# Splitting the level update of the first two tiles between VectorE and GpSimd in a linear-attention and GELU kernel

## The chip, the cores and the metric

The kernel runs on one core of one Trainium2 chip. The time is device microseconds of one execution. Five engines work side by side, each on its own queue of instructions in program order: TensorE (PE, whose weight loads are listed apart as PEld), VectorE (DVE), ScalarE (ACT), GpSimd (POOL) and SyncE (SP, which here only issues DMAs). They wait for each other through semaphores.

## The reference

Linear attention with decay per channel (4 batches, 8 heads, 768 positions, 48 channels), whose output feeds two matrix products with an exact GELU between them (3072 tokens, 384 to 2048 to 384):

```python
for t in range(S):
    kt, vt, rt, wt = (k[:, :, t], v[:, :, t], r[:, :, t], w[:, :, t])
    cur = np.einsum('bhd,bhe->bhde', u[None] * kt, vt)
    y[:, :, t] = np.einsum('bhd,bhde->bhe', rt, state + cur)
    state = wt[:, :, :, None] * state + np.einsum('bhd,bhe->bhde', kt, vt)
...
h = x @ w_in
g = 0.5 * h * (1.0 + erf(h * inv_sqrt2))
return (g @ w_out).astype(np.float32)
```

All inputs are float32, `w` lies between 0.8 and 0.95.

## The kernel before, in words

**Tiles.** The work is cut into 8 tiles `x` of 384 positions (a batch has two of them). `attention(x, unit)` makes the attention of a tile, `mlp(x)` its two products. While `mlp(x - 1)` runs, the attention of tile `x` is woven into it; the strings in `PLAN` say, letter by letter, which stream makes its next step, so the order of every engine's queue is written out by hand. In `PLAN[0]` there is no product to weave into: tile 0 runs as two units of half its heads each (streams `.` and `s`), beside the conversion of the weights (`c`) and the loads (`l`).

**Levels.** Inside a chunk of 64 positions the attention matrix is built in levels h = 1, 2, 4, 8, 16, 32 (`halves`, used for tiles 0 and 1 alone; the others use `quarters`). At each level

1. PE makes products `d` of `k` and `r` (L472) into PSUM,
2. `r` and `k` are multiplied in place by products of the decay `w` (`tot[h]`): of each stretch of 2h positions the later half of `r`, the earlier half of `k` (the update, L514 and L525),
3. the part of `d` that belongs to the level is copied into `a_sb`, under a mask by VectorE (L536) or, from h = 16, by ScalarE (L533).

The products of the next level wait for both halves of the update. After each product of tile 0 two matmuls over zeros (`keep_warm`, L242) follow on PE. Past the last level PE transposes `k` (L705), ScalarE copies that out (L707), PE makes `kv` (L731), VectorE chains the states (L746), and PE adds both parts of `y` (L772, L817); that last one reads the updated `r`.

**The update before.** Most updates are one VectorE product over both tensors (L525): the access patterns `rk` and `tt` step over `r` and `k` as an outer dimension of two, since both lie in one buffer (`bufs[0]` for tile 0, `bufs[1]` for tile 1). It takes 128 x 768 elements for a unit of tile 0 and 128 x 1536 for tile 1. In tile 0 at h = 1 and h = 32, `r` and `k` are already two products (L514, 128 x 384 each); that of `r` at h = 32 is put off until after the `kv` matmuls (`last_r`).

**What else is on VectorE there.** The weights arrive as 16 pieces of 64-bit floats. ScalarE makes three passes over each (L350, L351, L352), VectorE three more (L363, L365, L369). All the pieces are converted while tiles 0 and 1 run, and the products of `mlp(0)` (L1079, L1173) use them as they come. ScalarE takes its next piece only when VectorE has given a buffer back, and it also makes the GELU (L1082, L1084) that empties PE's PSUM banks.

**GpSimd** fills buffers and index patterns at the start, then fills `places` (L301, L306: a memset and four copies, into the end of the `w` of tile 0, so they wait for the level h = 1), and from tile 2 on issues DMAs that add (L990).

Of the kernel before, what the change touches and what calls it, by code (L numbers as in the profile page):

```python
# [72 lines left out]
def kernel(  # L73
# [25 lines left out]
    nc = tc.nc  # L99
# [185 lines left out]
    for i, h in enumerate(QUARTERS[:1]):  # L285
        for a in range(3):
            w_q = (3 - a) * C // 4
            z = q_ints[1 if a == 0 else 2]
# [84 lines left out]
    def attention(x, unit):  # L373
# [6 lines left out]
        n_u = qs * T  # L380
        base = unit * 3 * n_u
        r, k, w = (bufs[0 if x == 0 or i == 0 and x % 2 == 0 else 1][:, base + i * n_u:base + (i + 1) * n_u]
                   for i in range(3))
# [43 lines left out]
        for h in LEVELS:  # L427
            nb = n_u // (2 * h)
            t2 = tot[h].rearrange("p (n two) -> p n two", two=2)
# [35 lines left out]
        def products(bs, right, width, rest=False):  # L465
            d = pair("d")
            n = 0
            for b in bs:
                for i in range(NI):
                    for g in range(2):  # L470
                        for p in range(2):
                            nc.tensor.matmul(d[half[p], g, n * width:(n + 1) * width],  # L472
                                             lhsT=kc[half[g], b, i, p], rhs=right(half[g], b, i, p),
                                             start=True, stop=True)
                    n += 1
            if x == 0 and not rest:
                keep_warm(2)
            return d[:, :, 0:n * width]

        def diagonal():  # L480
            return [products([b], lambda z, b, i, p: rucs[b][z, i, p], C) for b in range(np_)]

        def copy_diagonal(diag):
            for b in range(np_):
                nc.vector.copy_predicated(out=at[:, :, b * NI:(b + 1) * NI],
                                          mask=masks[0].unsqueeze(1).unsqueeze(1).to_broadcast([128, 2, NI, C]),
                                          data=diag[b].rearrange("p g (i t) -> p g i t", t=C))

        def halves():

            for h in LEVELS:
                m = C // 2 // h
                if np_ < NPART:

                    d = products(range(np_), lambda z, b, i, p: rc[z, b, i, p], C, h == 1)
                    d = d.rearrange("p g (n m two j) -> p g n m two j", two=2, j=h, m=m)[:, :, :, :, 1, :]
                else:
                    right = rc.rearrange("p b i c (m two j) -> p b i c m two j", two=2, j=h)[:, :, :, :, :, 1, :]
                    d = products(range(np_), lambda z, b, i, p: right[z, b, i, p], C // 2)
                    d = d.rearrange("p g (n m j) -> p g n m j", j=h, m=m)  # L500
                if h == 1:
                    yield
                    diag = diagonal()
                yield

                r2 = r.rearrange("p (n two j) -> p n two j", two=2, j=h)[:, :, 1, :]
                t2 = tot[h].rearrange("p (n two) -> p n two", two=2)[:, :, 0:1].to_broadcast(r2.shape)
                k2 = k.rearrange("p (n two j) -> p n two j", two=2, j=h)[:, :, 0, :]
                tk = tot[h].rearrange("p (n two) -> p n two", two=2)[:, :, 1:2].to_broadcast(k2.shape)
                rk = bass.AP(tensor=r2.tensor, offset=r2.offset, ap=[r2.ap[0], [n_u - h, 2]] + list(r2.ap[1:]))  # L510
                tt = bass.AP(tensor=t2.tensor, offset=t2.offset, ap=[t2.ap[0], [1, 2]] + list(t2.ap[1:]))

                def update(z, r2=r2, t2=t2, k2=k2, tk=tk):
                    nc.vector.tensor_mul(*((k2, k2, tk) if z is k else (r2, r2, t2)))  # L514

                if x == 0 and m == 1:

                    update(k)
                    last_r.append(lambda: update(r))
                elif x == 0 and h == 1:  # L520
                    update(r)
                    yield
                    update(k)
                else:
                    nc.vector.tensor_mul(rk, rk, tt)  # L525
                yield
                ah = at.rearrange("p g n (m two j) -> p g n m two j", two=2, j=h)[:, :, :, :, 1, :]
                if h >= 16:

                    for p in range(2):  # L530
                        for i in range(m):
                            s = slice(p * 64 + i * 2 * h, p * 64 + i * 2 * h + h)
                            nc.scalar.copy(out=ah[s, :, :, i], in_=d[s, :, :, i])  # L533
                else:
                    mask = masks[h].rearrange("p (m j) -> p m j", j=h).unsqueeze(1).unsqueeze(1)
                    nc.vector.copy_predicated(out=ah, mask=mask.to_broadcast(ah.shape), data=d)  # L536
                if h == 1:
                    copy_diagonal(diag)
                yield
# [154 lines left out]

        last_r = []
        yield from halves() if x < 2 else quarters()


# [634 lines left out]
```

## Time and profile before

Three executions took 591.37, 592.99 and 596.03 us, median 592.99. The profiled execution's span is 591.7 us, with a mean granted PE clock of 0.997.

| engine | busy us | share of the span | instructions |
|---|---|---|---|
| PE | 575.3 | 97% | 7536 |
| PEld | 511.1 | 86% | 7536 |
| DVE | 436.3 | 74% | 835 |
| ACT | 281.4 | 48% | 648 |
| POOL | 51.5 | 9% | 57 |

The stages that hold the change, in us from the start of the span: tile 0 from the first product at 9.2 to its last `y` at 43.5, tile 1 from there to about 115. PE is busy for 31.3 of the first 43.5 us and, by the profile, for all of the time from 43.5 to 136.7; a busy PE is not PE at its peak, since matmuls are pipelined. GpSimd is busy for 8.0 us before 19 and for nothing from there to the first adding DMA.

Busy time of a group is listed with its mean for one instruction in ns. "Idle before" is the time that the engine stood still just ahead of these instructions, with what ended it. A wait put down to "issue" is one for which the profile shows no releaser.

### The profile page before, as it was taken

What the parts mean: (1) busy time and instruction counts of PE and PEld (TensorE: products, weight loads), DVE (VectorE), ACT (ScalarE), POOL (GpSimd) and SP (SyncE); (2) the same over time, 40 slices, a digit from 0 to 9 for tenths busy, and PEclk for the clock granted to TensorE, in tenths of its full rate; (3) what the DMA queues carried; (4) which work ended last, traced back from release to release, by engine and by line L of the source; (5) the groups of instructions that cost most, each with busy time, mean ns of one, the idle gap of its engine ahead of it and who ended that gap; (6) DMA issues with size and microseconds to landing.
All of it is one profiled execution on the core that took longest, in us unless ns stands there. A gap on an engine that the chain in (4) does not pass through costs nothing. (4 is left out here: it accounts for less than half of the span.)

```text
span 591.7 us, 17485 instructions
## 1 busy us (share of the span) xinstructions
PE 575.3 (97%) x7536; PEld 511.1 (86%) x7536; DVE 436.3 (74%) x835; ACT 281.4 (48%) x648; POOL 51.5 (9%) x57
## 2 busy tenths in 40 slices
PE   5879999999999999999999999999999999999997
PEld 3566666766799999999999999999999999999997
DVE  6979989998969886786859977686759977420332
ACT  2367889223612458046462368145560466435400
POOL 3100000000000130012100120003100111003100
PEclk8999999999999999999999999999999999999999
DMA  6758581020152532245232533334225232214200
GB/s 237 206 181 309 164 280 62 30 91 1 27 143 78 139 59 43 79 126 89 28 59 86 148 64 50 91 121 55 29 36 160 75 52 35 34 47 53 28 15 33
DMA packets 60797, 53.89 MB, mean 91 GB/s; under 512 B 32304, under 2 KB 45872, under 8 KB 60720
## 3 DMA queue, kind: packets, MB, share of 16 engines
q1 hardware_dynamic: 50832, 45.62, 25.6%
q0 software_dynamic: 9792, 7.08, 9.2%
q8 instruction: 59, 0.97, 0.7%
q14 instruction: 18, 0.15, 0.1%
q10 hardware_dynamic: 96, 0.07, 0.0%
HBM read 36.24 MB, written 4.72 MB: 69 GB/s over the span
## 5 line engine op out<-in xcount | busy, mean ns | idle before, releaser
L949 PE MATMUL h_ps<-xT,w_in_sb 128*128 128x192 f32 x480 | 95.4, 330 | 0.4 <-DVE o_sb L1216 0.4
L990 POOL DMA_DIRECT2D g<-o_sb x36 | 43.5, 1256 | 489.5 <-ACT o_sb L985 487.3
L949 PEld LDWEIGHTS h_ps<-xT,w_in_sb 128*128 128x128 f32 x480 | 79.7, 190 | 3.7 <-ACT g L981 1.5
L1079 PE MATMUL h_ps<-xT,w_in_sb 128*128 128x384 f32 x192 | 64.2, 490 | 0.0
L1079 PEld LDWEIGHTS h_ps<-xT,w_in_sb 128*128 128x128 f32 x192 | 35.8, 190 | 24.1 <-ACT kx L421 0.3
L1093 PE MATMUL o_ps<-w_out_sb,g 128*128 128x192 f32 x224 | 39.7, 326 | 0.0
L1093 PEld LDWEIGHTS o_ps<-w_out_sb,g 128*128 128x128 f32 x224 | 37.0, 190 | 0.3
L949 PE MATMUL u_ps<-s,w_in_sb 128*128 128x192 f32 x192 | 35.3, 327 | 0.0
L624 ACT COPY a_sb<-d 32x256 f32<-32x256 f32 (+8 forms) x90 | 32.6, 362 | 5.3 <-PE d L608 3.8
L472 PEld LDWEIGHTS d<-rkw 64*64 64x64 f32 x1152 | 19.8, 138 | 15.4 <-issue 9.7
L949 PEld LDWEIGHTS u_ps<-s,w_in_sb 128*128 128x128 f32 x192 | 31.7, 190 | 0.2
L992 DVE TENSOR_TENSOR g<-g,o_sb 128x384 f32<-128x384 f32 x12 | 6.6, 546 | 34.2 <-ACT o_sb L985 34.2
L641 DVE COPY_PREDICATED a_sb<-quarter,d 128x480 f32<-128x480 uint8 (+5 forms) x54 | 23.1, 438 | 11.6 <-PE d L608 10.3
L1093 PE MATMUL o_ps<-w_out_sb,f 128*128 128x192 f32 x176 | 31.6, 329 | 0.0
L1093 PE MATMUL o_ps<-t,g 128*128 128x192 f32 x176 | 31.4, 329 | 0.0
L1093 PE MATMUL o_ps<-w_out_sb,e 128*128 128x192 f32 x176 | 31.4, 329 | 0.0
L1093 PE MATMUL o_ps<-t,e 128*128 128x192 f32 x176 | 31.2, 328 | 0.0
L1093 PE MATMUL o_ps<-t,s 128*128 128x192 f32 x176 | 30.9, 327 | 0.0
L746 DVE SCALAR_TENSOR_TENSOR st<-st,tot_sb,kv_ps 128x48 f32<-128x48 f32 x160 | 29.0, 257 | 1.7 <-PE kv_ps L731 1.7
L1093 PEld LDWEIGHTS o_ps<-t,g 128*128 128x128 f32 x176 | 28.7, 190 | 0.4
L1093 PEld LDWEIGHTS o_ps<-w_out_sb,e 128*128 128x128 f32 x176 | 28.7, 190 | 0.3
L1093 PEld LDWEIGHTS o_ps<-w_out_sb,f 128*128 128x128 f32 x176 | 28.7, 190 | 0.3
(165 smaller groups left out, 1161.6 us busy)
## 6 DMA issues: line engine op xcount, KB each, us to landing
rkw<-in_rkw_dram SPq DMA_DIRECT2D x54, 256.0 KB, 4.0
g<-o_sb POOLq DMA_DIRECT2D x36, 192.0 KB, 3.6
raw<-in_w_out_dram SPq DMA_DIRECT2D x8, 768.0 KB, 4.4
v_in<-in_v_dram SPq DMA_DIRECT2D x8, 584.0 KB, 4.0
raw<-in_w_in_dram SPq DMA_DIRECT2D x5, 768.0 KB, 7.1
out_dram<-o_sb SPq DMA_DIRECT2D x20, 192.0 KB, 2.1
rkw<-kx SPq DMA_DIRECT2D x72, 48.0 KB, 2.1
rkw<-in_rkw_dram SPq DMA_DIRECT2D x6, 384.0 KB, 5.2
```

Source lines behind the costliest of these rows:

```text
L472: nc.tensor.matmul(d[half[p], g, n * width:(n + 1) * width], lhsT=kc[half[g], b, i, p], rhs=right(half[g], b, i, p), start=True, stop=True)
L624: nc.scalar.copy(out=at[z, g, first:behind, (a + 1) * h:], in_=d[z, :, :, to] if g == slice(None) else d[z, :, to])
L641: nc.vector.copy_predicated(out=an[:, :, :, :, (a + 1) * h:], mask=mask.to_broadcast(data.shape), data=data)
L746: nc.vector.scalar_tensor_tensor(out=stq[:, q, c], in0=stq[:, q, c - 1] if c else b4[:, q, NC - 1], scalar=totq[:, q, c:c + 1], in1=kvs[q ...
L949: nc.tensor.matmul(o, lhsT=lhsT, rhs=rhs, start=start, stop=True, skip_group_check=True)
L990: nc.gpsimd.dma_start(out=o, in_=z, accum_op=ALU.add)
L992: nc.vector.tensor_add(o, o, z)
L1079: nc.tensor.matmul(h_ps, lhsT=w_in_sb[:, f // FI, j, f % FI * 128:(f % FI + 1) * 128], rhs=xT[:, j, :], start=(j == 0), stop=(j == NJ - 1))
L1093: nc.tensor.matmul(o, lhsT=lhs(j), rhs=rhs(j), start=start and j == 0, stop=(j == HF - 1), skip_group_check=True)
```

## The change

In `halves` the combined product (L525) is gone, and with it the patterns `rk` and `tt`. `update(r)` is now issued on GpSimd, `update(k)` stays on VectorE, at every level of both units of tile 0 and of tile 1, the separate ones of h = 1 and h = 32 included.

```diff
-                rk = bass.AP(tensor=r2.tensor, offset=r2.offset, ap=[r2.ap[0], [n_u - h, 2]] + list(r2.ap[1:]))
-                tt = bass.AP(tensor=t2.tensor, offset=t2.offset, ap=[t2.ap[0], [1, 2]] + list(t2.ap[1:]))
 
                 def update(z, r2=r2, t2=t2, k2=k2, tk=tk):
-                    nc.vector.tensor_mul(*((k2, k2, tk) if z is k else (r2, r2, t2)))
+                    (nc.vector if z is k else nc.gpsimd).tensor_mul(*((k2, k2, tk) if z is k else (r2, r2, t2)))
...
                 else:
-                    nc.vector.tensor_mul(rk, rk, tt)
+                    update(r)
+                    update(k)
```

GpSimd's queue gets 18 products: 12 of 128 x 384 elements for tile 0, ahead of the memset and copies of `places`, and 6 of 128 x 768 for tile 1, behind them and ahead of the first adding DMA. VectorE's 8 products of 128 x 768 in tile 0 become products of 128 x 384, its 6 of 128 x 1536 in tile 1 become 128 x 768, and its four separate products of `r` in tile 0 are gone. The products `d` of PE now wait for VectorE and for GpSimd. The order of PE's, ScalarE's and SyncE's instructions is as it was. Lines below the change are one lower: L512 is the update, L535 the masked copy.

## The prediction

> **What bounds the kernel now.** First the page, for the busy tenths by slice. PE is full from the fourth slice on; VectorE is nearly full up to the eleventh.
>
> ```profile
> PE   5879999999999999999999999999999999999997
> DVE  6979989998969886786859977686759977420332
> ```
>
> Then busy time by stretch: tile 0's levels; three stretches of tile 1; the stretch up to tile 2's first product. The columns are the stretch, its length, and busy us of each engine.
>
> ```profile
> 15.10:33.20 18.10, 14.86 (x501) 9.52 (x501) 16.27 (x37) 7.96 (x15) 2.88 (x5) 1.00 0.76 224
> 43.50:62.00 18.50, 18.50 (x341) 12.19 (x338) 17.58 (x26) 13.49 (x25) 0.00 (x0) 1.00 0.74 259
> 62.00:80.00 18.00, 18.00 (x238) 11.38 (x238) 17.86 (x22) 15.04 (x29) 0.00 (x0) 1.00 0.68 234
> 80.00:100.00 20.00, 20.00 (x252) 13.01 (x251) 17.17 (x23) 18.55 (x28) 0.00 (x0) 1.00 0.36 120
> 100.00:136.70 36.70, 36.70 (x403) 24.59 (x401) 35.59 (x61) 13.05 (x25) 0.00 (x0) 1.00 0.21 71
> ```
>
> From 43.5 on PE never waits, so relief of VectorE there is worth nothing; but VectorE idles only 0.14 us of 18 between 62 and 80, and 2.83 of the next 20. Whatever blocks it eats that and then reaches PE. In tile 0 PE does stand still; its waits there are:
>
> ```profile
> PE d L472 <- issue: 1.4, 2, 0.9
> PE d L472 <- DVE e L365: 0.7, 1, 0.7
> PE d L472 <- DVE rkw L525: 0.5, 1, 0.5
> PE d L472 <- DVE rkw L178: 0.4, 1, 0.4
> ```
>
> The 1.4 is no engine's work. The 0.7 falls behind the first matmul of its product, and it is that one which waits for VectorE, so no update ends it. The 0.5 and the 0.4 (a memset just behind an update) are updates that came late. So at most 0.9 us can be gained in tile 0, and nothing after it.
>
> **What is saved.** VectorE's own rows, from the groups by shape:
>
> ```profile
> L525 DVE TENSOR_TENSOR rkw<-rkw,tot_sb 128x1536 f32<-128x1536 f32 x5 | 8.8, 1752 | 1.0 <-PE d L472 1.0
> L525 DVE TENSOR_TENSOR rkw<-rkw,tot_sb 128x768 f32<-128x768 f32 x8 | 7.7, 966 | 1.0 <-PE d L472 1.0
> L514 DVE TENSOR_TENSOR rkw<-rkw,tot_sb 128x384 f32<-128x384 f32 x4 | 2.1, 554 | 0.8 <-PE d L472 0.8
> L431 DVE TENSOR_TENSOR tot_sb<-rkw 128x768 f32<-128x768 f32 x2 | 1.9, 954 | 0.0
> ```
>
> A unit's update goes from 966 to 554 ns, 0.4 us less, eight times; a level of tile 1 goes from 1.75 to 0.95 us, 0.8 less, six times, 4.8 us in all. The four lone products of `r`, 0.55 each, leave VectorE too; the last two (34.67 to 35.7) stood ahead of 1.46 us of idle time and were worth nothing.
>
> **What the product costs on GpSimd.** No row shows a two-input product there. The nearest are its memsets, 93 ns for one element and 525 for 512, that is 0.84 ns an element; and the four copies of 128 elements (L306), at 401 ns the shortest and 414 the median, so (401 - 93) / 128 = 2.41 ns an element with one input. Lower bound, the memset's rate: 0.42 us for 384 elements, 0.74 for 768. At the copy's rate: 1.02 and 1.94. Upper bound, the copy's rate once for each input: 1.94 and 3.79. I take 1.1 and 2.1, next to the copy, the nearest row, and a little above it for the second input. [...]
>
> **Whether both engines can run at once.** The fourth copy of L306 took 1127 ns. It met a VectorE product that reads two inputs from SBUF; the two rows of the timeline, start and length:
>
> ```profile
> 17.61 1.13 POOL L306 COPY rkw<-ident 32x128 f32<-32x128 f32 x1
> 17.50 0.95 DVE L525 TENSOR_TENSOR rkw<-rkw,tot_sb 128x768 f32<-128x768 f32 x1
> ```
>
> The product ends at 18.45 and the copy at 18.74, 0.29 later: most of the copy's work came after it. The copies ahead of it ran beside a masked copy (L485), whose data is in PSUM, at the usual 0.4 us. So GpSimd reads stand behind VectorE products with two SBUF inputs. I take it that VectorE stands behind GpSimd in the same way when GpSimd comes first; no row shows that. [...]
>
> **Tile 0.** A round is a level of both units. The four rounds from 15.13 to 30.27 take 3.37, 3.60, 4.58 (0.94 of issue and the 0.5 wait in it) and 3.59 us. With r and k of a unit one behind the other, a round needs 2 x (1.1 + 0.55 + 0.1 to hand over) = 3.5 us, about what it has, because the masked copies (1.0 or 0.57) cover the next r. That cover is gone from 27.5 on, where L363, L365 and L369 (0.55, 0.95, 0.95) fill VectorE: the four r of h = 16 and 32 hold it up for 4 x 1.1 = 4.4 us. Off that come 2 x 0.4 saved, its own idle time of 0.61 and 0.15, and the 0.73 between the last k (to 33.41) and the second half of the transposes (34.14): 2.1 us late, and the transposes with it. Bounds: -0.9 at the memset's rate; at 1.94, rounds of 5.2 and a tail of 5.5 with some of both in common, +9. I take +2.1.
>
> **Tile 1.** r of each level is ready when its `d` ends, when VectorE is in a conversion; GpSimd takes its turn at the end of that instruction, and what is queued on VectorE (the rest of the piece, then k, then the masked copy) waits 2.1 us. ScalarE waits for VectorE's buffers, with the GELU behind it in its queue, and PE for both. Six levels: 6 x 2.1 - 4.8 = 7.8 us. VectorE's idle time from 62 to the last level's k (95.86) absorbs about 2.8, and k then has 0.8 (it ended at 97.62, the transposes ran from 98.41): 4.2 us late there, and PE after that goes without a wait, so it is kept to the end. From level to level the next `d` begins 5.9 us or more after the last one's end, so r itself is no wait. Bounds: 0 at 0.74 (4.4 blocked, 4.8 saved); +14.3 at 3.79.
>
> **Moved without a price.** GpSimd's memset and copies of `places` start behind tile 0's last r, near 36 instead of 15.65; tile 2 reads them at 136.7, and 100 us cover them (3 us without that). The adding DMAs come after all 18 products. SP's order is unchanged; its loads of weights are released by memsets (L219) that stand between the updates and move with them by some tenths.
>
> **Sum.** +2.1 + 4.2 = +6.3 us. The profiled execution's span of 591.7 becomes 598.0; it lies 1.3 below the median of the runs, 592.99, so the forecast is 599.3.
>
> **Rivals.** First, GpSimd does not hold VectorE up: it yields at once, or both run. For it: no row shows VectorE waiting for GpSimd, and L525 at 17.50 started while the third copy ran and still took 0.95. Against: the block is plain in the other direction. Then tile 1 gains nothing, as PE never waits, and tile 0 gains at most 0.9: 592.1, not slower. It decides if VectorE's rows keep their lengths and starts where r runs. Second, VectorE always goes first and r is starved to its gaps. If k of h = 16 in tile 1 (86.39) beats its r, VectorE has no gap and no masked copy until about 95.1; r ends at 97.2, where `d` should start at 94.19: +3. Tile 0, with its copies for cover, about +1: 597. Against: GpSimd is idle as `d` ends, and VectorE mostly is not. Third, GpSimd's strides and second read cost the upper bound: +9 and +14.3, 616. For it: the copy, which writes with a step of 16 bytes, is almost three times a memset for each element. Against: past h = 1, r lies in runs of two to 32 elements.
>
> **How the numbers follow.** 1% is 5.9 us, about what a measurement here can tell from no change: over 598.9 is slower. Forecast 0.52, from 596 (r at 0.95 and 1.7) to 606 (1.5 and 2.8), 0.40 of it over 598.9; no hold-up 0.22; starved 0.10; upper bound 0.14; a gain by something not seen 0.02. Slower 0.40 + 0.14, and a hundredth of the starved case, 0.55; same 0.12 + 0.22 + 0.09 = 0.43; faster 0.02, since all the waits an update could end are 0.9 us. The range 591.5 to 609 leaves out the lowest part of the no hold-up case and most of the upper bound, about 0.2.
>
> **What will show it.** r on GpSimd near 1.1 and 2.1 us, longer where it starts inside a VectorE product. VectorE rows (L365, L369, the update) longer, or starting later, where they meet r. k of tile 1's last level 4 to 5 us later relative to PE's own queue, and a PE wait ahead of the transposes near 98, or before it behind ScalarE. From 137 on the same trace, shifted. Wrong if VectorE's rows stay at 0.95 with no gaps ahead of them, or if PE waits for GpSimd itself.

## The result, and the profile after

Nine executions each: before 593.1 us (591.14 to 596.03), after 597.42 us (595.89 to 599.2), a ratio of 1.0062 with a 95% interval of 1.0044 to 1.0081. The change costs 4.3 us, in the direction forecast and two thirds of the size (+6.3). It stays under the 598.9 from which the prediction counts a result as slower, so what came is its case "same" (0.43) and not "slower" (0.55), though the interval is clear of 1. The parts of the sum are another matter.

The profiled execution, the slowest of the nine, has a span of 597.4 us (+5.7 on that of the execution profiled before). The page again, now with the granted clock:

```profile
PE   6779999999999999999999999999999999999998
...
DVE  5678999998969977786759977697768977520332
...
PEclk8889999999999999999999999999999999999999
```

PE's second slice (15 to 30 us) has lost a tenth, and the clock reads 8 in the first three slices, up to 45 us and so nearly all of tile 0 (before, in the first alone). The stretches of the prediction (those of tile 1 shifted by about 4 us; us, then busy us of PE, PEld, VectorE, ScalarE and GpSimd with their instructions, granted clock, DMA share, GB/s):

```profile
15.10:33.20 18.10, 14.58 (x409) 9.30 (x412) 12.12 (x29) 7.33 (x12) 8.59 (x8) 0.81 0.66 195
47.20:66.20 19.00, 18.38 (x339) 11.93 (x336) 18.62 (x25) 12.64 (x24) 4.18 (x2) 1.00 0.72 249
66.20:84.20 18.00, 18.00 (x238) 11.28 (x237) 17.86 (x20) 15.46 (x29) 3.82 (x3) 1.00 0.56 181
84.20:104.20 20.00, 19.94 (x251) 12.73 (x250) 19.86 (x24) 18.93 (x30) 3.92 (x2) 1.00 0.48 169
```

In tile 0 the granted clock fell from 1.00 to 0.81 and PE got through 409 matmuls in place of 501. In tile 1 VectorE's busy time in the last of these stretches rose from 17.17 to 19.86 of 20 us, and PE is full all the same. PE's waits from the first product to tile 2 (us in all, times, longest):

```profile
PE d L472 <- issue: 3.1, 2, 2.2
PE kv_ps L730 <- issue: 2.3, 1, 2.3
PE kt_ps L704 <- DVE rkw L512: 0.8, 1, 0.8
PE y_ps L771 <- DVE st L745: 0.6, 1, 0.6
PE h_ps L1078 <- ACT xT L823: 0.6, 1, 0.6
PE d L472 <- POOL rkw L512: 0.4, 1, 0.4
```

The waits of the products `d` for VectorE's updates are gone (0.5 and 0.4) and 0.4 for GpSimd's came; the transposes wait 0.8 for VectorE's k, and "issue" went from 1.4 + 1.4 to 3.1 + 2.3. GpSimd's products and VectorE's, by shape:

```profile
L512 POOL TENSOR_TENSOR rkw<-rkw,tot_sb 128x384 f32<-128x384 f32 x10 | 11.7, 1168 | 10.3 <-PE d L472 6.4 <-issue 1.8 <-DVE a_sb L535 1.4
L512 POOL TENSOR_TENSOR rkw<-rkw,tot_sb 128x768 f32<-128x768 f32 x5 | 9.7, 1948 | 37.0 <-PE d L472 29.7 <-issue 7.3
```

```profile
L365 DVE SCALAR_TENSOR_TENSOR e<-raw,e 128x768 uint32<-128x768 uint32 x16 | 18.9, 1179 | 0.0
...
L512 DVE TENSOR_TENSOR rkw<-rkw,tot_sb 128x768 f32<-128x768 f32 x5 | 7.4, 1484 | 0.0
```

r takes 1.17 and 1.95 us (taken: 1.1 and 2.1). L365 had a mean of 953 ns before and has 1179 now, and the update of k in tile 1, 950 ns by itself, has 1484: VectorE does stand behind GpSimd. One such meeting, by the timeline (start, length):

```profile
73.70 1.75 POOL L512 TENSOR_TENSOR rkw<-rkw,tot_sb 128x768 f32<-128x768 f32 x1 [7.42 <-PE d L472]
73.88 2.39 DVE L365 SCALAR_TENSOR_TENSOR e<-raw,e 128x768 uint32<-128x768 uint32 x1
```

GpSimd's r ends at 75.45 and VectorE's instruction, which takes 0.95 alone, ends at 76.27, 0.82 later. Each of the six r of tile 1 met one VectorE instruction in this way; what that one took beyond its usual length was 1.92, 1.67, 1.44, 1.37, 1.34 and 1.30 us, 9.0 in all.

Three marks of PE's own queue give the difference by stage: the first product of tile 0, the first product of `mlp(0)` (about 3 us after tile 0's last y; the first level of tile 1 lies between), the first transpose of tile 1's k, and the first product of tile 2.

| stage | before, us | after, us | difference |
|---|---|---|---|
| start to first product | 9.20 | 9.11 | -0.09 |
| tile 0 | 37.45 | 41.69 | +4.24 |
| tile 1 to its transposes | 51.76 | 52.04 | +0.28 |
| transposes to tile 2 | 38.29 | 39.02 | +0.73 |
| the rest | 455.00 | 455.54 | +0.54 |

So +4.2 stands in tile 0 and +1.0 in tile 1: the reverse of the forecast's +2.1 and +4.2.

**What "issue" is.** Counted in order, with its instructions that only wait for semaphores, PE has these waits at numbers 706, 962 and 1730 before the change, multiples of 256 apart, and the 0.7 us that the profile puts down to L365 stands at 1218, on the same grid. The other profiles have them at some of the same numbers; the traces of experiments 1 to 8 hold 14 matmuls fewer, so there the numbers come out up to 13 lower. The queue that the page calls "q8 instruction" moved 59 packets of 16,384 bytes each, and 59 x 256 = 15,104, close to PE's 15,229 records (15,072 matmuls and weight loads, 157 semaphore waits). Where PE waits at such a number, it goes on 1.1 to 1.6 us after one of these packets has landed. From the grid of 256, the count of 59 and these times I take it that a packet holds PE's next 256 instructions, and that PE waited for them; no row says so by itself. From the trace, in us:

```
kernel, instruction   packet moves     PE stops   PE goes on   stands
before,  962          22.34 to 23.59   24.07      25.01        0.94
after,   962          23.78 to 24.72   23.82      26.02        2.20
before, 1730          37.46 to 38.41   38.40      39.77        1.37
after,  1730          40.28 to 41.24   40.44      42.70        2.26
```

**What followed.** In these traces the granted clock keeps a value for 3.41 us or a multiple of that (after the change, 0.50 from 8.70 to 12.12, from 25.77 to 32.60 and from 42.84 to 46.25). Such stretches around these two stops (columns as above):

```profile
22.36:25.77 3.41, 1.46 (x54) 0.83 (x43) 0.71 (x3) 0.00 (x0) 1.61 (x2) 1.00 0.95 330
25.77:29.19 3.42, 2.76 (x53) 1.74 (x57) 1.97 (x5) 1.98 (x3) 1.19 (x1) 0.50 0.08 28
29.19:32.60 3.41, 3.41 (x87) 2.33 (x80) 2.08 (x4) 2.01 (x6) 1.17 (x1) 0.50 0.56 124
39.43:42.84 3.41, 1.15 (x76) 1.03 (x72) 1.94 (x12) 1.91 (x3) 0.43 (x1) 1.00 0.13 47
42.84:46.25 3.41, 3.41 (x100) 3.41 (x98) 2.23 (x13) 0.79 (x1) 0.00 (x0) 0.50 0.27 58
```

PE was busy for 1.46 and 1.15 of 3.41 us, and had half its clock in what came next: three stretches, 10.2 us at half clock, worth up to 5.1. Before, tile 0 had none after its first products.

### The profile page after: what moved, and what is told of

Its sections match the earlier page's. It is cut to its first block, busy times and chain, and to the rows that moved or that the text cites. A ratio compares the mean times of both kernels' runs of the same rounds, so it can differ in the third digit from the quotient of the medians.

```text
span 597.4 us, 17536 instructions
## 1 busy us (share of the span) xinstructions
PE 579.0 (97%) x7536; PEld 513.7 (86%) x7536; DVE 437.8 (73%) x831; ACT 281.1 (47%) x648; POOL 77.4 (13%) x75
## 5 line engine op out<-in xcount | busy, mean ns | idle before, releaser
L472 PEld LDWEIGHTS d<-rkw 64*64 64x64 f32 x1152 | 21.0, 147 | 16.3 <-issue 13.3
L472 PE MATMUL d<-rkw 64*64 64x64 f32 (+1 forms) x1152 | 23.7, 235 | 7.0 <-DMA rkw<-in_rkw_dram 3.5
L745 DVE SCALAR_TENSOR_TENSOR st<-st,tot_sb,kv_ps 128x48 f32<-128x48 f32 x160 | 29.0, 257 | 1.7 <-PE kv_ps L730 1.6
```

The source lines that it names most:

```text
L472: nc.tensor.matmul(d[half[p], g, n * width:(n + 1) * width], lhsT=kc[half[g], b, i, p], rhs=right(half[g], b, i, p), start=True, stop=True)
L745: nc.vector.scalar_tensor_tensor(out=stq[:, q, c], in0=stq[:, q, c - 1] if c else b4[:, q, NC - 1], scalar=totq[:, q, c:c + 1], in1=kvs[q ...
```

## The experiments

The theories that the expectations speak of:

- **H**, the forecast's: VectorE stands behind GpSimd, and what is queued behind it reaches PE, in the tail of tile 0 (h = 16 and 32) and in tile 1.
- **F**: VectorE gets ahead in tile 0 and releases loads sooner; PE's instruction packets queue behind these, PE stands longer for them, and loses half its clock after that.
- **G**: GpSimd is late with r, and PE waits for it.

All runs had five rounds: 12 executions of each kernel (6 of the eleventh) beside 29 to 35 of the kernel before on the same chip. The first four share a chip, so do the next four and the last four.

**1 and 2. One tile at a time.**

```diff
# tile 0 only
+ (nc.vector if z is k or not (x == 0) else nc.gpsimd).tensor_mul(...)
# tile 1 only
+ (nc.vector if z is k or not (x == 1) else nc.gpsimd).tensor_mul(...)
```

In the other tile the combined product stays.

> GpSimd makes r in tile 0 alone; tile 1 has its combined product on VectorE again. Theory H (hold-up: VectorE stands behind GpSimd's reads, tile 1 is where that costs most): +2 us over the kernel before or less, the larger part of the changed kernel's +4.3 gone. Theory F (fetch: PE stands still for its own instructions in tile 0, because GpSimd lets VectorE run ahead and release the loads sooner, and the clock falls behind that): +2.5 to +3.5, a wait of PE put down to issue of 1.5 us or more near 24 or near 40, with half clock behind it in some executions.

> GpSimd makes r in tile 1 alone; tile 0 is as before. Theory H: +4 us. Theory F: +1 to +2, all of it between 98 and 115 us (the transposes and the matmuls that wait for the states), with tile 0 the same as before to 0.5 us. In both, VectorE rows that meet a GpSimd product take 2.1 to 2.4 us in place of 0.55 to 0.95.

Measured: tile 0 alone 596.13 us against 593.09, ratio 1.0049 (1.0025 to 1.0072), +3.0. Tile 1 alone 594.69, ratio 1.0023 (1.0006 to 1.0040), +1.6. Tile 0 is the dearer part, so H has the weights wrong. In the profile of tile 1 alone, tile 0 is no longer than before (36.46 us, no half clock after its first products), and one new wait reaches PE, the same as after the change:

```profile
PE y_ps L775 <- DVE st L749: 0.6, 1, 0.6
```

The stage from the transposes to tile 2 takes 39.02 us there, as after the change, against 38.29; the way to the transposes 51.87 against 51.76. The trace shows +0.8 for tile 1; the time's +1.6 holds that in its interval.

**3. The split without GpSimd.** Both halves as products of VectorE, two in place of one. In effect:

```diff
- nc.vector.tensor_mul(rk, rk, tt)
+ nc.vector.tensor_mul(r2, r2, t2)
+ nc.vector.tensor_mul(k2, k2, tk)
```

> Both parts on VectorE, as two products at every level of both tiles: the split without GpSimd. VectorE gets 2 x 0.55 in place of 0.97 us eight times in tile 0 (+1.1 in all) and 2 x 0.95 in place of 1.75 six times in tile 1 (+0.9). Theory H: +0.5 to +1.5, since VectorE's time is what counts. Theory F: between -1 and +1, the waits for issue in tile 0 as before (0.9 and 1.4) or shorter, since the loads are released later.

Measured: 593.71, ratio 1.0006 (0.9990 to 1.0023). More instructions on VectorE are no cost that shows. The +0.6 lies in the range of either theory.

**4. The change once more**, on the chip of 1 to 3.

> The changed kernel as it is, for a second profile and more times beside the other three. Both theories: +4.3 us over the kernel before, within 1 us. Theory F: the waits for issue in tile 0 differ from those of the first profile by up to 1 us, and an execution without half clock behind them is 2 to 3 us shorter than 597.4.

Measured: 596.0, ratio 1.0038 (1.0020 to 1.0055), +2.9. Its profile is of an execution with one stretch of half clock in tile 0 after the first products, in place of three: tile 0 took 37.81 us there, where the profile above has 41.69. It is the same kernel, so the 4 us between them are no work of an engine. Tile 1's two stages are 51.88 and 39.03, as above.

**5 and 6. Without the loads of tile 1's r, k and w,** after and before the change. These kernels leave out that load (L179) and compute tile 1 on a constant.

```diff
- dma.dma_start(out=bufs[1][:, s], in_=rkw[1, :, s])
+ nc.gpsimd.memset(bufs[1], 0.5)
```

> The changed kernel without the loads of tile 1's r, k and w (8 DMAs of 288 KB during tile 0): that tile works on constants. Theory F: with those DMAs gone the fetches of PE's instructions come in time; the waits for issue in tile 0 fall from 0.9 + 2.2 + 2.3 us to under 1 us each, no half clock follows, and the kernel is within 2.5 us of the kernel before without these loads. Theory H: VectorE is held up as before, so it stays 4 us or more over the kernel before without these loads.

> The kernel before without the same loads: the control of the other. Theory F: its own waits for issue in tile 0 (0.5 + 0.9 + 1.4 us) shrink too, so it gains 1 to 2.5 us over the kernel before. Theory H: no statement on it beyond some tenths.

Measured: 594.74 (1.0024, 1.0008 to 1.0041) and 591.99 (0.9977, 0.9964 to 0.9991); between them 2.75 us. That is under H's 4 and a little over F's 2.5, and about the change's own cost on another chip (+2.9 in 4), so the loads of tile 1 are part of it at most. The kernel before gained 1.5 us, as F expected, but not by the waits that F named: those are 1.1, 0.7 and 1.9 us in place of 0.5, 0.9 and 1.4. After the change they are 1.4, 1.1 and 2.0 us, not under 1, and half the clock followed the last. One packet does follow these loads. In both kernels nothing is loaded between instruction 1218 and the packet after it, and that packet starts 1.2 and 1.0 us after PE has passed; in the profiles before and after the change, 1,055 and 1,011 KB are moved first, and it starts 3.64 and 3.22 us after.

**7 and 8. The levels of tile 0 apart:** GpSimd's r at h = 1 to 8, and at h = 16 and 32; tile 1 as before.

```diff
+ (nc.vector if z is k or not (x == 0 and h <= 8) else nc.gpsimd).tensor_mul(...)
# and, in the other kernel
+ (nc.vector if z is k or not (x == 0 and h >= 16) else nc.gpsimd).tensor_mul(...)
```

> GpSimd makes r in tile 0 at h = 1 to 8 alone, where masked copies cover it and VectorE is not yet in the weights. Theory H: -0.9 to +0.5 us, since the hold-up lies in the last two levels. Theory F: the loads are still released sooner, so +1 to +3 us, with the wait for issue near 24 longer than 0.9 in some executions, and less at 40.

> GpSimd makes r in tile 0 at h = 16 and 32 alone, where L363, L365 and L369 are on VectorE too. Theory H: +2 us, VectorE's L365, L369 or its product of k lengthened by 0.6 or more, and PE waiting 0.8 for k ahead of the second half of the transposes. Theory F: +0.5 to +2; the wait near 24 as before (0.9), the one of the kv matmuls near 40 over 1.8 in place of 1.4, because the gate of the loads there stands behind a VectorE row that is held up.

Measured: 595.62, ratio 1.0035 (1.0015 to 1.0055), +2.1 for h = 1 to 8; 593.7, ratio 0.9997 (0.9980 to 1.0015), +0.2 for the tail. That refutes H in tile 0: its price was all in the tail, and the tail is free (F had +0.5 or more there). In the profile of h = 1 to 8, these are PE's longest waits from 15 to 50 us:

```profile
PE d L472 <- issue: 2.3, 2, 1.4
PE kv_ps L734 <- issue: 2.0, 1, 2.0
PE d L472 <- POOL rkw L514: 1.1, 1, 1.1
```

The 1.1 is at h = 8, where the updates of both units stand one right behind the other; PE waited 0.5 there for VectorE before, and 0.7 to 0.8 in 2, 3, 6 and 8. That is G, for 0.3 to 0.6 us. After the 2.0 in kv, half the clock was gone from 38.57 to 41.98.

**9. No r at all in tile 0.** This kernel leaves out the r half of tile 0's updates; tile 1 is that of the change.

```diff
+ if x == 0 and z is not k:
+     return
```

> This kernel leaves out the r half of every level update in tile 0 (12 products of 128 x 384), so tile 0's later levels are products of r as it was; VectorE makes the k products there as in the changed kernel, and tile 1 is that of the changed kernel. GpSimd does nothing in tile 0 but places, so PE cannot wait for it and it cannot hold VectorE up there. Theory G (what tile 0 costs is GpSimd's lateness: PE's waits for r of 1.1 us at h = 8, and the hold-up): tile 0 is then worth nothing or a small gain, since every update is 0.4 us shorter and nothing replaces it; with tile 1's +1.6 the time is 592.5 to 594.5, +0 to +1.5 over before. Theory F (what it costs comes from VectorE running ahead: loads released sooner, PE at its next 256 instructions before they are there, half a clock after it): the cost stays although work is left out, +3 to +4.5, 595.5 to 597.5, with waits put down to issue of about 2 us in tile 0, and a half-clock stretch between 20 and 50 us in about half of the executions (granted clock under 0.9965 in 5 to 8 of 12).

Measured: 594.7, ratio 1.0025 (1.0006 to 1.0044), +1.5: what tile 1 costs by itself (1.0023), and nothing for tile 0. It lies 0.2 above the range of G and 0.8 below that of F, and no stretch after the first products of its profile has half the clock. VectorE has less to do in tile 0 here than in any other kernel, so its lead alone does not bring the cost about. That GpSimd's r is needed for it follows only within the noise: each of the two ratios is good to about 1.1 us, and this kernel also leaves out work and waits of PE.

**10. GpSimd's r at h = 1, 2 and 4 only,** which avoids the place at h = 8.

```diff
+ (nc.vector if z is k or not (x == 0 and h <= 4) else nc.gpsimd).tensor_mul(...)
```

> GpSimd makes r in tile 0 at h = 1, 2 and 4 only; h = 8, 16, 32 of tile 0 and all of tile 1 are as before. The kernel with h = 1 to 8 cost +2.1 (1.0035). Theory G: the cost is the place at h = 8 where the updates of both units stand one after the other and PE waits 1.1 us for the second r: without it +0 to +0.8, 593.0 to 594.0. Theory F: three levels of four still run ahead, so +1.2 to +2, 594.3 to 595.3, with a wait put down to issue of 1.8 us or more in tile 0.

Measured: 595.09, ratio 1.0032 (1.0016 to 1.0048), +1.9, in F's range and above G's. PE waits for GpSimd nowhere in this profile, and it has two stretches of half clock, each behind a stop for a packet:

```profile
24.03:27.44 3.41, 1.69 (x60) 1.13 (x64) 1.54 (x4) 0.08 (x1) 1.13 (x3) 1.00 0.56 200
27.44:30.86 3.42, 3.42 (x83) 2.18 (x76) 2.79 (x7) 3.36 (x6) 0.00 (x0) 0.50 0.48 102
37.69:41.10 3.41, 1.55 (x87) 1.43 (x79) 2.04 (x13) 2.64 (x3) 0.00 (x0) 1.00 0.02 5
41.10:44.51 3.41, 3.41 (x69) 3.27 (x66) 2.42 (x11) 0.54 (x2) 0.00 (x0) 0.50 0.52 179
```

The kernel without r, experiment 9, around its own two longest stops:

```profile
22.57:25.98 3.41, 1.92 (x77) 1.29 (x80) 1.07 (x4) 0.00 (x0) 0.00 (x0) 1.00 0.94 328
25.98:29.39 3.41, 3.30 (x125) 2.20 (x125) 2.85 (x8) 2.50 (x3) 0.00 (x0) 1.00 0.16 26
36.22:39.63 3.41, 1.94 (x126) 1.81 (x120) 2.52 (x15) 1.33 (x2) 0.00 (x0) 1.00 0.10 35
39.63:43.04 3.41, 2.89 (x117) 2.75 (x110) 3.04 (x14) 1.78 (x3) 0.00 (x0) 1.00 0.52 180
```

PE stood for 1.49 and 1.47 us of these, not 1.72 and 1.86 as with r at h = 1 to 4, and kept its clock.

**11 and 12. Other loads first:** h = 1 to 8 as in 7, and the kernel before, both with the weights' second piece ahead of tile 1's shares and three load steps of tile 0 about 20 steps later.

```diff
-    0: ".lls.....sslsc.lsslll.sl.sls..sl.lscsl..sss.lscs.lscs.s.clll.s..s.cccsss...wss..ss.ff",
+    0: ".lls.....sslsc.lsslll.sl.ss..s.scsl..sss.lscs.lscs.s.cllllll.s..s.cccsss...wss..ss.ff",
...
- chain(weight_in(0, True), islice(second, 5), weight_in(1, True), second, weight_in(2, True))
+ chain(weight_in(0, True), weight_in(1, True), second, weight_in(2, True))
```

> The kernel with GpSimd's r in tile 0 at h = 1 to 8 (+2.1, 1.0035), with the loads in another order: the weights' second piece before tile 1's r, k and w, and three of the load steps of tile 0 some 20 steps later, past the level h = 8. Theory F: fewer loads stand ahead of PE's instruction packets between 17 and 30 us, so the cost falls to 0 to +1 against the same order without the change (e12_before_late), and the half clock is rarer (4 of 12 or fewer). Theory G: the loads' order matters nothing to the update, so the difference to e12_before_late stays +1.5 to +2.5.

> The kernel before with the same later loads, the control to e11_h8_late. Theory F: PE's waits put down to issue in tile 0 (1.4 us in the products, 1.4 in kv) shrink a little: -1 to 0, 592.0 to 593.2. Theory G says nothing of it: 0 +- 0.6. If the later weights hold ScalarE or VectorE up, +0.5 or more.

Measured: 598.49 (1.0088, 1.0058 to 1.0118) and 594.69 (1.0035, 1.0013 to 1.0057). Both theories missed: the order is dearer by itself, and the difference between the two medians, 3.8 us, is larger than either said (by the ratios it is 3.1, give or take 2.2, so it does not tell them apart). Moved, the loads go ahead of another packet. In 12, 926 KB go ahead of the packet for kv, which starts 3.16 us after PE has passed instruction 1474 (before: 78 KB, 1.14 us); PE stands for 3.29 us at 36.39, 2.13 of them in one stretch:

```profile
37.55:40.96 3.41, 1.28 (x68) 1.28 (x69) 0.95 (x5) 0.85 (x2) 0.00 (x0) 1.00 0.19 62
40.96:44.37 3.41, 3.41 (x68) 3.28 (x68) 2.34 (x11) 2.27 (x4) 0.00 (x0) 0.50 0.51 170
```

Its profile is the one without GpSimd's r that lost its clock there, and so shows the second half of F with no help from GpSimd. No kernel of the twelve that computes the whole is faster than the one before.

**All profiles side by side.** Half clock is counted from 15 us to the end of tile 0; the longest stand is the most that PE stood still in one stretch of 3.41 us there. The last column counts executions whose mean granted clock is under 0.9965; one stretch at half clock takes 0.5 x 3.41 / 592 = 0.0029 off, and one at the first products is common, so these have at least two, or most of them.

| kernel | tile 0, us | half clock, us | longest stand, us | low clock |
|---|---|---|---|---|
| before | 37.45 | 0 | 1.09 | 6/35, 13/35, 8/29 |
| 2, tile 1 only | 36.46 | 0 | 1.26 | 1/12 |
| 3, two on VectorE | 37.49 | 0 | 1.32 | 4/12 |
| 6, before, no load | 35.58 | 0 | 1.54 | 1/12 |
| 8, h = 16 and 32 | 37.94 | 0 | 1.73 | 3/12 |
| 9, no r | 36.69 | 0 | 1.49 | 2/12 |
| 12, before, later loads | 37.85 | 3.41 | 2.13 | 8/12 |
| after | 41.69 | 10.24 | 2.26 | 6/9 |
| 1, tile 0 only | 41.95 | 10.24 | 2.34 | 8/12 |
| 4, the change again | 37.81 | 3.41 | 2.20 | 6/12 |
| 5, after, no load | 38.58 | 3.41 | 2.00 | 3/12 |
| 7, h = 1 to 8 | 38.26 | 3.41 | 2.02 | 6/12 |
| 10, h = 1 to 4 | 38.54 | 6.83 | 1.86 | 8/12 |
| 11, 7 with later loads | 39.66 | 3.41 | 1.65 | 6/6 |

The seven profiles with GpSimd's r at the early levels of tile 0 have a tile 0 of 39.5 us in the mean, the other seven 37.1: +2.4. Their half clock (with that of the first products, 8.7 to 13 us) is 7.7 and 2.3 us in the mean; half of the difference is 2.7. So in these profiles the lost clock is as large as the difference of tile 0.

A profile is one execution, and the times of all executions with their clocks say less. With (1 - granted clock) x time as the most that the clock can have cost, in us of the means over the kernel before on the same chip:

| kernel | longer by | lost clock, at most | the rest |
|---|---|---|---|
| 1, tile 0 only | 3.3 | 2.4 | 0.9 |
| 7, h = 1 to 8 | 1.75 | 0.45 | 1.3 |
| 10, h = 1 to 4 | 1.7 | 1.0 | 0.7 |
| 2, tile 1 only | 1.4 | -0.1 | 1.5 |
| 4, the change | 2.8 | 0.85 | 1.9 |

The rest is good to about 1 us either way. At a granted clock of 1.00 throughout, five executions of the change took 595.2 us in the mean and three of the kernel with h = 1 to 8 took 594.8, against 592.9 (sixteen) and 592.7 (eleven) of the kernel before. So half clock is at most a quarter to three quarters of what tile 0 costs; the rest comes without it.

## Why the prediction was right or wrong

The direction was right, and the range held the time, but neither term of the sum held. Tile 0's +2.1 was too small, against +3.0 by the times of 1 and +4.2 in the profile; tile 1's +4.2 was too large, against +1.6 by the times of 2 and +1.0 in the profile. That the errors took from each other, and the total came within 2 us, is luck.

- **r's duration: right.** 1.17 and 1.95 us for 1.1 and 2.1. The bounds from the memset and from two copies were far; the copy row was the near one.
- **The hold-up: right in kind.** That VectorE stands behind GpSimd was taken over from the other direction; no row of the profile before shows it. Here L365 (2.39 and 2.32 for 0.95 us), the update of k (2.29 and 2.25 for 0.95) and even L363, which reads one tensor (2.22 for 0.55 us at 64.48), stood behind GpSimd until r was through. The two rivals that deny it, no hold-up and starved, are out, and so is the upper bound (r at 1.94 and 3.79). The other direction hardly shows in tile 0: seven r start inside VectorE's product of k, some 0.1 us behind its start, and take 1.16 to 1.24 us, against 1.17 for the first r, which met nothing. "Longer where it starts inside a VectorE product" did not come about there: that GpSimd stands behind VectorE's products, read from one copy before the change (1.13 us at 17.61), is not borne out by these seven.
- **Tile 1, +4.2: mis-sized.** The term "6 x 2.1" had the whole of r as lost to VectorE; it lost 9.0, not 12.6 us. With the 4.8 saved, the 2.8 of idle time and the slack of 0.8 that the prediction took off, 0.6 is left; the stages show +0.28 and +0.73, the times +1.6 (0.4 to 2.4). It also came out elsewhere: 0.6 us at the wait of y for the states (L745), behind the transposes, not ahead of them.
- **Tile 0's tail, +2.1: wrong.** "The four r of h = 16 and 32 hold it up for 4 x 1.1 = 4.4 us" did happen in part: L369 took 1.60 and a k 1.16, and the transposes waited 0.8 for k. But the kernel that has only this costs 0.2 us. After the tail PE runs into the packet for kv whatever it does: it stopped there in every profile, so an earlier or later arrival changes how long it stands, and less when it goes on. That this hides the tail was argued from the profiles, not tried by itself.
- **Tile 0's rounds, "about what it has": the step that failed.** The levels h = 1 to 8 cost +2.1. The prediction put the 1.4 of issue down as "no engine's work", which was so, and then held it constant, with the clock at 1.00. Both moved: PE's longest stop for a packet grew from 1.4 us (at kv) to between 1.9 and 2.4, and half the clock followed in the profile of each of the seven kernels. The 0.7 that the prediction read as a wait for VectorE is such a stop too, at instruction 1218: it ends 1.3 us after a packet has landed.
- **PE waiting for GpSimd**, named as what would prove the forecast wrong, occurs once in a profile, at h = 8, in the six where GpSimd makes that r in tile 0: 0.4 to 1.1 us, in place of 0.5 to 0.8 for VectorE. The term was left out.

**What is shown and what stays open.** Shown: tile 0's cost comes from h = 1 to 8 (+2.1 against +0.2 for the tail); in the profiles the half clock follows stops for instruction packets; and the load order alone can bring both about (12). Argued: that it needs GpSimd's r (9), and that half clock is its larger part. Open: by what path GpSimd's r makes these stops longer, and what makes the rest of the cost. Loads ahead of the packet are the likeliest path: for the kv packet, 78 to 274 KB go with a start 0.9 to 1.1 us after the pass of instruction 1474 (before, 2, 3), 456 to 688 KB with 1.7 to 2.1 (after, 1, 4 to 8, 10, 11), 926 with 3.2 (12). But experiment 9 has 436 KB and 1.15 us, and while the loads run the KB grow with the wait itself, so they do not tell cause from effect. Nor does every late packet have much loaded ahead of it: behind instruction 962 it started 2.8, 2.5 and 2.7 us after the pass in the profiles after, of 1 and of 11, with under 60 KB ahead. There, and in 4 and 7, it came 0.3 us after PE's wait for GpSimd at h = 8 had ended; no run tries that apart. And the change's cost itself, +4.3 in one set and +2.9 in another, is a mean over executions that lose no, one or three such stretches.

## What to carry to other kernels

A wait that is "nobody's work" was not a constant here (the 1.4 us at the kv products became 2.3): look at where PE's stops fall in its instruction count (here 256 apart) and how much of each clock stretch (here 3.41 us) they fill. Here stands of 1.49 and 1.47 us kept the clock (9), and stands of 1.72 and 1.86 were each followed by a stretch at half of it (10), worth up to 1.7 us (0.5 x 3.41). Work moved to an engine that VectorE then stands behind can cost VectorE more than it saves; here 9.0 us of hold-up came for 4.8 us saved. And a hold-up on an engine off the path is taken off its idle time first (here 2.8 us): count that before calling it a cost.

## What the hardware showed that was not expected

- **PE's clock was halved after stretches that PE stood still for about half.** Of 199 stretches of 3.41 us between 12 and 60 us in 14 profiles, the nine in which PE stood 1.86 us or more were all followed by half the clock, of five with 1.65 to 1.73 two were, and of the 185 below 1.6 only two, which were at half clock themselves. 1.86 us is 54% of such a stretch.
- **A PE instruction packet has a price of its own.** From PE's passing of one mark it took 0.5 us (2, behind 1218) to 4.1 us (after, behind 706) to the start of the packet for the next, about 1 us for the packet and 1.1 to 1.6 us more; PE was at that mark 4.2 us (from 706) or 2.1 us (from 1474) after the one before.
- **A VectorE instruction of one tensor stood behind GpSimd too** (L363, 2.22 for 0.55 us). It is one row: at 81.25 us an L363 that started 0.02 us behind an r took its usual 0.55.
